# New priorities for the first blocks' operations, and maxima over partitions by a matmul whose stationary operand repeats the column

## The chip, the cores and the metric

The kernel runs on one core of one Trainium2 chip. The metric is the time of one execution on the device in microseconds (us), as the median of several runs. The engines are named as in the profile: PE is TensorE, DVE is VectorE, ACT is ScalarE, POOL is GpSimd, and SP is SyncE, which here only issues transfers.

## The reference

Three layers follow each other. The first is attention over keys and values that are averaged in groups of 8 positions, the second a dense two-layer network with a leaky activation, the third a network of 8 experts of which each token uses the one with the largest logit.

```python
# attention: B, H, S, D = 8, 8, 576, 64;  pool = 8;  Sp = 72
k_p = k.reshape(B, H, Sp, pool, D).mean(axis=3)
v_p = v.reshape(B, H, Sp, pool, D).mean(axis=3)
scores = scale * np.matmul(q, k_p.transpose(0, 1, 3, 2))
...
x = attn @ v_p                          # to (4608, 512)
h = x @ w_in                            # 512 -> 2048
g = np.maximum(h, 0.0) + alpha * np.minimum(h, 0.0)
x = g @ w_out                           # 2048 -> 512
...
logits = x @ w_gate                     # 8 experts
expert_idx = np.argmax(logits, axis=1)
...                                     # for each expert e and its tokens xe:
ye = np.maximum(xe @ w1[e], 0.0) @ w2[e]
out[mask] = gate_w[mask, None] * ye
```

## The kernel before

**Tiles and stages.** The 4608 tokens are 36 tiles of 128 and 18 blocks of two tiles. Every f32 operand of a large matmul is split into a high and a low f16 half, and three products of halves are added up. A split needs a power of two as a scale, and this needs a maximum over the operand. For a batch (`plan_batch`, 8 of them) K and V are loaded in slices into two buffers (`raw`), pooled (L450 on VectorE, L454 to L456 on GpSimd), scaled and split, and K is transposed by a DMA (`kT`, L483). For a tile (`plan_tile`) q is loaded, split and transposed by a DMA, then come scores (L572), maximum (`smax`), bias (`nb`, L583), exponentials (L591), a transposition by DMA (L622), the product with V (L631), and the split result xT. The tiles of the first two blocks need batch 0 alone; tile 4, the first of block 2, needs batch 1 too.

**The dense layer.** `plan_w` loads w_in and w_out in 8 chunks each, and puts each chunk together from integer parts (ScalarE L726 to L735, VectorE L738 and L742). It takes the chunk's maximum (L190), and once the maximum is there splits it into a high (`hi`) and a low half (`lo`, L210 on VectorE, L212 and L213 on GpSimd). w_in has four groups of two chunks with a scale each; w_out has one scale, so nothing of w_out is split before all 8 chunks have their maxima. `plan_in` computes a block's first layer (hp, L822: 16 parts of 12 matmuls), with the activation on ScalarE (L836) and VectorE (L840), and splits the result into gT. `plan_out` computes a tile's second layer (yp, L869: 4 parts of 12). Then come the gate and, beside all this, the scaling of the experts' weights (`plan_expert`). When the blocks are through, the expert slots follow (L1301, L1319).

**The maximum over partitions.** `over_all` (L308 to L332) takes a column with one maximum for each partition and returns the largest of the 128 in every partition. It masks the column to the bits of the exponent (L315), multiplies an identity matrix by it (`diag`, L320, VectorE, into the tile dg), and multiplies a matrix of ones with that diagonal on TensorE (L324, into the tile mp), so that every partition holds all 128 values. Then it reduces them (L327). It is called for alpha and the gate (a pair of columns), each batch (a pair; batch 0 in two calls), each w_in group, w_out, and each expert weight.

**The order of the work.** Nothing is issued as the program text runs. Each step is an operation of `Plan`, added with its engine or a choice of engines, an estimated duration, its inputs, a key and the buffers it takes and frees. `Plan.emit` plays the operations through with these estimates. At each step it takes, over all engines, the operation that can start first; among several that could start at the same time on an engine, the one with the smallest key goes first. The order found so is the order of each engine's queue. `PEN` is a handicap in us for each engine of a choice, and `lk` marks operations that share a port with GpSimd in the estimate. The operations are numbered in the order in which they are added. Keys of a block's first layer are 16j (j below 2) or 32j plus the part; `first` shifts some keys below 70.

## Time and profile before

| what | us |
|---|---|
| median of 3 runs | 1355.64 |
| lowest and highest of them | 1351.82, 1360.56 |
| the profiled execution | 1353.38 |
| its span, first to last instruction | 1351.7 |
| TensorE busy (91% of the span) | 1233.8 |
| VectorE busy (69%) | 935.2 |
| ScalarE busy (43%) | 585.4 |
| GpSimd busy (27%) | 361.8 |

The chain that ended last reaches back from the end only to 1011.67 us, through the expert slots' matmuls and scatters, so it tells nothing of the first blocks. The stages up to 300 us are read from tables by stage and from timelines. Wait times that are named behind an instruction are the idle time of its engine just before it, and what ended it.

### The profile page before, as it was taken

Reading aid. Unit: us, or ns where it says so; the run is one execution under the profiler, and the core shown is the slowest. Engines: PE = TensorE matmul, PEld = TensorE weight load, DVE = VectorE, ACT = ScalarE, POOL = GpSimd, SP = SyncE. Lnnn points to the kernel's source line nnn. Section 1 sums busy time; section 2 is a strip of 40 time slices with the busy share of each in tenths; the row PEclk is TensorE's granted clock in tenths of the full one; section 3 lists DMA queues with packets and bytes.
Section 4 is the critical chain, followed back from the end, with each engine's and each line's share of the span. In section 5 each row is a group of like instructions: output and inputs, shape, how many; then the busy total and the mean of one; then the engine's idle time right before and its main releaser. Section 6 shows DMA issues by size and latency. Waiting matters only on the chain. (4 is left out here: it accounts for less than half of the span.)

```text
span 1351.7 us, 30262 instructions
## 1 busy us (share of the span) xinstructions
PE 1233.8 (91%) x11555; PEld 862.0 (64%) x11555; DVE 935.2 (69%) x2268; ACT 585.4 (43%) x1342; POOL 361.8 (27%) x378
## 2 busy tenths in 40 slices
PE   0058599999999999999999999999999999999997
PEld 0046456657766776677657766776767677776775
DVE  6999998989998998989979976853432332322322
ACT  2797735556754665467546654731111110110100
POOL 4265233124244142112334202220211222121211
PEclk9998799999999999999999999999999999999999
DMA  9994386797887897987877678394489433883316
GB/s 236 281 238 134 71 214 199 158 209 198 217 184 161 219 210 148 215 158 178 220 179 203 144 188 180 78 298 132 111 238 251 84 84 74 251 267 72 86 49 216
DMA packets 314789, 237.71 MB, mean 176 GB/s; under 512 B 258383, under 2 KB 267727, under 8 KB 309776
## 3 DMA queue, kind: packets, MB, share of 16 engines
q1 hardware_dynamic: 301184, 215.46, 63.3%
q0 software_dynamic: 7552, 20.23, 4.8%
q8 instruction: 92, 1.51, 0.5%
q10 hardware_dynamic: 5904, 0.04, 0.3%
q14 instruction: 57, 0.47, 0.2%
HBM read 263.52 MB, written 54.87 MB: 236 GB/s over the span
## 5 line engine op out<-in xcount | busy, mean ns | idle before, releaser
L822 PE MATMUL hp<-xT,w_in_hl 128*128 128x256 f16 x3456 | 394.5, 275 | 6.8 <-DVE r L840 4.1
L869 PE MATMUL yp<-w_out_hl,gT 128*128 128x512 f16 x1728 | 383.9, 380 | 0.0
L822 PEld LDWEIGHTS <-w_in_hl 128*128 128x128 f16 x3456 | 335.8, 99 | 50.4 <-DVE r L840 4.6
L869 PEld LDWEIGHTS <-gT 128*128 128x128 f16 x1728 | 166.4, 98 | 193.3 <-issue 1.4
L1301 PEld LDWEIGHTS <-ws 128*128 128x128 f16 x3744 | 210.7, 98 | 5.8 <-issue 1.2
L1301 PE MATMUL hp<-x2gT,ws 128*128 128x128 f16 x3744 | 212.5, 219 | 1.0 <-ACT hr L1307 1.0
L1319 PE MATMUL op<-ws,ht 128*128 128x512 f16 x936 | 205.6, 379 | 0.5 <-issue 0.5
L1307 ACT ACTIVATE hr<-hp 128x512 f32<-128x512 f32 x78 | 46.2, 597 | 352.4 <-PE hp L1301 321.6
L1319 PEld LDWEIGHTS <-ht 128*128 128x128 f16 x936 | 90.5, 98 | 106.3 <-issue 0.9
L840 DVE SCALAR_TENSOR_TENSOR r<-r,al,hp 128x256 f32<-128x256 f32 x288 | 123.9, 471 | 8.6 <-ACT r L836 8.4
L1311 DVE CAST ht<-hr 128x512 f16<-128x512 f32 x78 | 33.7, 432 | 136.8 <-ACT hr L1307 135.1
L1326 DVE TENSOR_SCALAR so<-op,cb 128x512 f32<-128x512 f32 x39 | 29.3, 751 | 141.5 <-PE op L1319 138.2
L836 ACT ACTIVATE r<-hp 128x512 f32<-128x512 f32 x144 | 86.9, 604 | 90.0 <-PE hp L822 73.1
L591 ACT ACTIVATE e<-sc,nb,esc 128x72 f32<-128x72 f32 x288 | 116.4, 419 | 6.9 <-DVE inv L289 5.0
L195 ACT ACTIVATE eo<-ew,es 128x512 f16<-128x512 f32 x128 | 88.9, 723 | 65.3 <-DMA wsc<-eo 29.2
L1010 POOL DMA_INDIRECT table<-rec,pu x36 | 40.6, 1128 | 265.2 <-DVE pu L1007 142.0
L450 DVE TENSOR_REDUCE kp<-raw 72x64 f32<-72x512 f32 (+1 forms) x90 | 100.0, 1112 | 16.5 <-DMA raw<-in_k_dram 9.3
L848 ACT ACTIVATE gT<-r 128x512 f16<-128x512 f32 x144 | 91.5, 636 | 29.6 <-DVE r L840 15.8
L853 DVE TENSOR_TENSOR gT<-r,gT 128x512 f16<-128x512 f32 x142 | 100.7, 711 | 3.7 <-ACT gT L848 3.3
L1329 POOL DMA_INDIRECT out_dram<-so,srec x39 | 39.7, 1018 | 194.1 <-DVE cb L1324 93.9
L1276 POOL DMA_INDIRECT x2g<-x2d,srec x41 | 43.7, 1067 | 167.1 <-DMA srec<-table 61.3
L190 DVE TENSOR_REDUCE em<-ew 128x1 f32<-128x1024 f32 x64 | 76.7, 1206 | 0.0
(217 smaller groups left out, 1259.2 us busy)
## 6 DMA issues: line engine op xcount, KB each, us to landing
ws<-wsc SPq DMA_DIRECT2D x166, 1024.0 KB
ew<-in_moe_w_dram SPq DMA_DIRECT2D x32, 1024.0 KB
wsc<-eo SPq DMA_DIRECT2D x64, 512.0 KB
x2d<-x SPq DMA_DIRECT2D x36, 256.0 KB
qr<-in_q_dram SPq DMA_DIRECT2D x32, 256.0 KB
w_in_f<-in_moe_w_in_dram SPq DMA_DIRECT2D x16, 512.0 KB
w_out_f<-in_moe_w_out_dram SPq DMA_DIRECT2D x16, 512.0 KB
raw<-in_k_dram SPq DMA_DIRECT2D x56, 144.0 KB
```

Source lines behind the costliest of these rows:

```text
L190: V.tensor_reduce(out=o, in_=i, axis=axis, op=ALU.max, apply_absolute_value=True)
L195: A.activation(out=hi, in_=src, func=ACTF.Copy, scale=s)
L450: V.tensor_reduce(out=o_, in_=r.rearrange("p h (r d) -> p h d r", r=PL), axis=AX.X, op=ALU.add)
L591: A.activation(out=c["e"][x], in_=c["scv"][x], func=ACTF.Exp, bias=c["nb"][:, z // 4, z % 4:z % 4 + 1], scale=c["esc"], accum_out=c["sm"][x])
L822: T.matmul(out=hp, lhsT=wt[:, a, kk, (m % 4) * 128:(m % 4 + 1) * 128], rhs=xTt[j][:, x, kk, :], start=(n == 0), stop=(n == 3 * KD - 1))
L836: A.activation(out=c["r"], in_=hps[j, m // 2], func=ACTF.Relu, scale=-1.0)
L840: V.scalar_tensor_tensor(out=c["r"][:, z], in0=c["r"][:, z], scalar=al1[:, m - 1 + z:m + z], in1=hps[j, m // 2][:, z], op0=ALU.mult, op1=A ...
L848: A.activation(out=gT[j][0][:, n2], in_=c["r"], func=ACTF.Copy)
L853: on(eng).tensor_tensor(out=gT[j][1][:, n2], in0=c["r"], in1=gT[j][0][:, n2], op=ALU.subtract)
L869: T.matmul(out=ypt[i], lhsT=gT[j][x][:, m, o_ * 128:(o_ + 1) * 128], rhs=W["w_out"][part][:, w, m % 4, :], start=(m == 0 and x == 0 and w ...
L1301: T.matmul(out=hp[:, f, :], lhsT=ws[kk // 2][:, kk % 2, a, ff * 128:(ff + 1) * 128], rhs=c["xT"][:, x * KD + kk, :], start=(z == 0), stop= ...
L1319: T.matmul(out=op, lhsT=c["ht"][:, x, f, :], rhs=ws[f // 4][:, f % 4, w, :], start=(f == 0 and x == 0 and w == 0), stop=(f == KF2 - 1 and ...
```

## The change

**Keys and engines by number.** A table `KEYS` adds a shift to the keys of 92 operations, and `SIDE` fixes the engine of 9 that have a choice, by a handicap of 99 us on the others. The numbers count the operations of the new program, which has no `diag`. By the order of the calls they are these:

- 41 to 72: batch 1's loads of slices (keys down by about 5 to 7) and poolings. The poolings of K slices 2, 4, 5, 6 and 7 go from 14, 16, 17, 18 and 19 to 40.0, 44.8, 44.7, 36.8 and 31.0; those of V slices 3 to 6 from 23 to 26 up to 39.7 to 46.0; the last from 27 to 17.6. Each pooling also waits for the one before it, as in the old program.
- 80 to 137: a copy and V's low half of batch 1, loads and poolings of batches 2 and 3. 395 to 605: operations of tiles 1 to 9, among them splits of q, maxima, first exponentials and scales.
- 1321 to 1374: w_in's second chunk, two steps of its scales. 1412: the maximum of w_out's first chunk, 22 to 72.5. 1436 to 1448: w_out's sixth chunk, and the maximum over the chunks (27 to 15.9).
- 1472 to 1625: activations and splits of blocks 0 to 2, and the yp parts 2 and 3 of tile 2 (1576, 1577: 52 and 54 to 88.9 and 170.7). 1630 and 1631: yp parts of tile 4. 2478 to 2515: expert 0's loads, maxima, splits and a store. 2994 to 3036: gate matmuls and their reductions of blocks 0 and 1.
- `SIDE`: GpSimd for poolings of batches 2 and 3 (100, 112, 134), V's low half of batch 2 (130), the low half of w_out's second chunk (1457), and two splits of block 2 (1592, 1605); VectorE for one pooling of batch 1 (54) and one split of expert 0 (2506).

**The maximum over partitions.** `diag` and its tile go. The matmul takes as stationary operand the upper 16 bits of the masked f32 column, read as bf16 and repeated 128 times with step 0, and the identity as moving operand; a pair of columns takes two matmuls.

**Order between operations.** A q maximum waits, in the plan, for the scales of the tile four before. Scores and products of a tile that ends a batch come after those of all earlier tiles. The low halves of w_in and w_out follow each other, a block's last yp part comes after that of its first tile, and the store of x2d is dated from the split instead of the transpose before it.

```diff
@@ -34,8 +34,26 @@
+KEYS = {
+    11: 33.24, 41: -4.95, 43: -4.95, 45: -4.95, 46: 26.02, 47: -4.95, 49: -4.91, 50: 28.84, 51: -4.91, 52: 27.68, 53:
+    -6.76, 54: 18.82, 55: -6.76, 56: 12.02, 57: -6.8, 59: -6.8, 64: 16.68, 66: 22, 68: 16.98, 70: 18.33, 72: -9.43,
+    80: -3.31, 84: -9.06, 87: -4.35, 89: -4.35, 91: -5.5, 93: -5.75, 95: -2.35, 97: -2.82, 99: -2.27, 101: -2.27, 105:
+    -3.95, 110: 37.67, 115: 7.45, 118: 27.69, 119: 27.74, 124: 52.02, 130: -12.61, 137: -16.16, 395: 71.78, 401:
+    -57.07, 415: 27.13, 421: 66.26, 425: -127.75, 432: 4.88, 447: 71.14, 451: -3.83, 456: 63.31, 461: -25.55, 475:
+    9.79, 485: -124.46, 499: 59.65, 501: -8.17, 530: -68.36, 544: -72.1, 551: -64.63, 555: -18.52, 605: -33.03, 1321:
+    -101.78, 1322: -93.78, 1323: -60.6, 1365: 26.95, 1374: 25.36, 1412: 50.46, 1436: -101.23, 1437: -18.51, 1448:
+    -11.12, 1472: -1.09, 1487: 36.95, 1496: 37.83, 1555: 14.78, 1576: 36.9, 1577: 116.72, 1594: 9.08, 1625: 5.36,
+    1630: -94.27, 1631: -30.36, 2478: 137.61, 2481: 45.47, 2484: 27.95, 2495: -60.74, 2497: -51.38, 2498: 65.41, 2505:
+    -63.32, 2506: -125.52, 2507: -56.94, 2514: -13.19, 2515: 60.24, 2994: 46.2, 2996: -31.62, 2998: 45.68, 3036: 39.29
+}
+SIDE = {
+    54: "DVE", 100: "POOL", 112: "POOL", 130: "POOL", 134: "POOL", 1457: "POOL", 1592: "POOL", 1605: "POOL", 2506:
+    "DVE"
+}
 class Op:
-    __slots__ = ("eng", "dur", "fn", "deps", "key", "lat", "acq", "rel", "n", "users", "est", "end", "kind", "lk")
+    __slots__ = ("eng", "dur", "fn", "deps", "key", "lat", "acq", "rel", "n", "users", "est", "end", "kind", "lk", "pen")
@@ -50,7 +68,12 @@
         o = Op()
+        at = len(self.ops)
+        key += KEYS.get(at, 0)
         o.lk = lk
+        o.pen = PEN.get(eng)
+        if at in SIDE:
+            o.pen = tuple(0.0 if x == SIDE[at] else 99.0 for x in eng)
         o.kind = kind
@@ -94,7 +117,7 @@
                     if isinstance(o.eng, tuple):
-                        t += PEN[o.eng][o.eng.index(name)]
+                        t += o.pen[o.eng.index(name)]
                     if pick is None or (t, k, i) < pick[:3]:
@@ -250,7 +273,7 @@
     pools = dict(att=5, raw=2, kp=2, kc=1, KT=2, VS=2, vlo=1, q=3, qs2=1, qT=2, sc=1, e=2, A=1, AT=1, xT=2, wst=WST, wst2=WST2, big=15,
-                 h=3, r=2, y=2, x2=3, x2T=2, gps=1, dg=1, ew=4, eo=2, rec=3, so=2, srec=8)
+                 h=3, r=2, y=2, x2=3, x2T=2, gps=1, ew=4, eo=2, rec=3, so=2, srec=8)
     plan = Plan(pools)
@@ -314,21 +337,17 @@
-        def diag():
-            d["g"] = wk.tile([128, 2, 128], BF16, tag="dg", name="dg", bufs=1)
+        def mm():
+            h = get().bitcast(BF16)
+            d["p"] = ps_g.tile([128, 2, 128], F32, tag="g", name="mp")
             for z in range(n):
-                V.tensor_scalar(out=d["g"][:, z], in0=idb, scalar1=get()[:, z:z + 1], scalar2=None, op0=ALU.mult)
-        def mm():
-            d["p"] = ps_g.tile([128, 2, 128], F32, tag="g", name="mp")
-            T.matmul(out=d["p"][:, 0:n], lhsT=ones, rhs=d["g"][:, 0:n], start=True, stop=True)
+                T.matmul(out=d["p"][:, z], lhsT=h[:, 2 * z + 1:2 * z + 2].to_broadcast([128, 128]), rhs=idb, start=True, stop=True)
...
         o = chain("DVE", [mask], deps + [o_c1], key)
-        o = add("DVE", 0.17 * n, diag, [o], key=key, lat=0.05, acq=[("dg", 1)], lk=True)
-        o = add("PE", 0.07 * n, mm, [o], key=key - 1000, acq=[("gps", 1)], lat=0.15, rel=[("dg", 1)])
+        o = add("PE", 0.07 * n, mm, [o], key=key - 1000, acq=[("gps", 1)], lat=0.15)
         return add("DVE", 0.1 + 0.14 * n, red, [o], key=key - 1000, lat=0.05, rel=[("gps", 1)])
@@ -530,7 +549,7 @@
-    xTt, oX, oXh = {}, {}, {}
+    xTt, oX, oXh, oSC, oAV, oQM = {}, {}, {}, {}, {}, {}
     KC = (128, 3 * SP_ - 128)
@@ -643,16 +662,17 @@
         o = add("SP", dmat(262144) * 1.85, load, kind="q", key=first(dl - 30, -6), acq=[("q", 1), ("att", 1)])
-        o = add("DVE", dve(512), q1, [o], key=dl - 18)
+        o = add("DVE", dve(512), q1, [o], order=[oQM.get(i - 4)], key=dl - 18)
         o = chain("DVE", pow2s(lambda: (c["m"], c["inv"], c["s"])), [o], dl - 18)
-        o_s = o
+        o_s = oQM[i] = o
         o = add(ANY, his(512), q2, [o], key=dl - 17, acq=[("qs2", 1)], lk=True)
...
         o_e = add("DVE", tiny(len(bs)), esc, [o_s] + [oSK[b] for b in bs], key=dl - 13, lk=True)
-        o = add("PE", pe(16 * len(bs), SP_), scores, [o] + [oKT[b] for b in bs], key=dl - 13, acq=[("sc", 1)],
+        o = add("PE", pe(16 * len(bs), SP_), scores, [o] + [oKT[b] for b in bs], order=[oSC.get(x) for x in range(i) if ends], key=dl - 13, acq=[("sc", 1)],
                 rel=[("qT", 1)] + [("KT", 1)] * len(ends))
+        oSC[i] = o
         o = add("DVE", dve(576), smax, [o], key=dl - 12)
@@ -664,8 +684,9 @@
         o = add("SP", 1.8, aT, [o1, o2], kind="AT", key=dl - 7 - SPA, acq=[("AT", 1)], rel=[("A", 1)])
-        o = add("PE", pe(16, 128), av, [o] + [z for b in bs for z in oVS[b]], key=dl - 4, acq=[("gps", 1)],
+        o = add("PE", pe(16, 128), av, [o] + [z for b in bs for z in oVS[b]], order=[oAV.get(x) for x in range(i) if ends], key=dl - 4, acq=[("gps", 1)],
                 rel=[("AT", 1)] + [("VS", 1)] * len(ends))
+        oAV[i] = o
         o = oXh[i] = add("ACT", act(512), xhi, [o, oXh.get(i - 1)], key=dl - 3, acq=[("xT", 1)] if half == 0 else [])
@@ -784,7 +805,7 @@
-        p1 = None
+        p1 = p2 = None
         for c in range(8):
@@ -803,7 +824,7 @@
             o = p1 = add(ANY, his(1024), hi, [o_sc, p1], key=first(key - 1, 122), acq=[("big", 1)] if c % 2 == 0 else [], lk=True)
-            o = add(EITHER, stt(1024), lo, [o], key=first(key - 1, 91), rel=[("big", 1)] if c % 2 == 1 else [], lk=True)
+            o = p2 = add(EITHER, stt(1024), lo, [o], order=[p2], key=first(key - 1, 91), rel=[("big", 1)] if c % 2 == 1 else [], lk=True)
             oW[name] += [o, o]
@@ -870,7 +891,7 @@
             oY[i] = add("PE", pe(12, DM), mm, [oG[j, 2 * part], oG[j, 2 * part + 1]] + oW["w_out"][4 * part:4 * part + 4]
-                        + [oY.get(i) if part else None],
+                        + [oY.get(i) if part else None], order=[oY.get(i - 1) if last and o_ else None],
                         key=key_out(i) + 2 * part, acq=[("y", 1)] if part == 0 else [],
@@ -909,9 +930,10 @@
             o = add("DVE", dve(512), y3, [o], key=k_, rel=[("y", 1)])
+            o_y = o
             o = add("SP", 1.0, y4, [o], kind="yT", key=k_ - SPY, acq=[("x2T", 1)])
             oT.append(o)
-            oS.append(add("SP", dmat(262144), y5, [o], kind="x2", key=k_ + 1, rel=[("x2", 1)]))
+            oS.append(add("SP", dmat(262144), y5, [o_y], order=[o], kind="x2", key=k_ + 1, rel=[("x2", 1)]))
```

## Rows read from the trace of the kernel before

**Rows 1.** Page, 40 slices: busy tenths of TensorE.

```profile
PE   0058599999999999999999999999999999999997
```

**Rows 2.** By stage: length; PE, PEld, DVE, ACT, POOL busy; clock, DMA share, GB/s.

```profile
0.00:87.67 87.67, 7.98 (x103) 6.26 (x104) 71.07 (x125) 55.72 (x96) 35.61 (x48) 1.00 0.98 264
87.67:144.34 56.67, 49.77 (x423) 40.84 (x420) 55.14 (x106) 43.01 (x73) 29.86 (x24) 0.94 0.51 130
144.34:165.14 20.80, 4.56 (x99) 4.09 (x98) 19.93 (x47) 13.80 (x42) 3.52 (x3) 0.64 0.31 73
165.14:300.00 134.86, 132.78 (x967) 80.87 (x964) 122.47 (x290) 68.39 (x156) 34.30 (x34) 0.99 0.76 194
300.00:1351.70 1051.70, 1038.74 (x9977) 729.98 (x9975) 666.57 (x1703) 404.48 (x978) 258.50 (x271) 1.00 0.67 171
```

**Rows 3.** Timeline of TensorE: start, us, work, wait before.

```profile
87.67 7.63 PE L822 MATMUL hp<-xT,w_in_hl 128*128 128x256 f16 x48
...
127.22 17.19 PE L822 MATMUL hp<-xT,w_in_hl 128*128 128x256 f16 x156
...
144.34 1.12 PE L572 MATMUL sc<-KTb,qT 128*64 128x72 f16 x32
...
163.09 1.11 PE L572 MATMUL sc<-KTb,qT 128*128 128x72 f16 x16 [6.95 <-ACT e L591]
...
165.14 11.59 PE L869 MATMUL yp<-w_out_hl,gT 128*128 128x512 f16 x48
...
177.25 5.35 PE L869 MATMUL yp<-w_out_hl,gT 128*128 128x512 f16 x24
```

**Rows 4.** Timeline of VectorE, from the last w_out chunks to yp.

```profile
148.79 2.35 DVE L738 SCALAR_TENSOR_TENSOR w_out_t<-wc,w_out_t 128x1024 int32<-128x1024 int32 x2
...
154.31 0.10 DVE L315 TENSOR_SCALAR iw<-iw 128x1 int32<-128x1 int32 x1
...
155.58 0.24 DVE L320 TENSOR_SCALAR dg<-idb,iw 128x128 bf16<-128x128 bf16 x1
...
156.61 0.28 DVE L327 TENSOR_REDUCE mr<-mp 128x1 f32<-128x128 f32 x1
...
162.29 1.28 DVE L210 SCALAR_TENSOR_TENSOR w_out_hl<-w_out_t,cg,w_out_hl 128x1024 f16<-128x1024 f32 x1 [0.25 <-ACT w_out_hl L195]
```

**Rows 5.** Table by stage, the diagonal products of L320 alone.

```profile
0.00:165.14 165.14, 6.42 (x11) 0.93 0.74 194
165.14:1351.70 1186.56, 6.36 (x28) 1.00 0.68 173
```

**Rows 6.** Tiles dg and mp: min/median/max ns, first and last start.

```profile
L324 PE MATMUL mp<-dg,ones x31: 219/219/372, 19.1 to 851.9; 128*128 128x128 bf16 x23, 128*128 128x256 bf16 x8
...
L320 DVE TENSOR_SCALAR dg<-idb,m x16: 233/245/254, 202.7 to 849.2; 128x128 bf16<-128x128 bf16 x16
```

**Rows 7.** Batch 1's pooling on VectorE, and SyncE's transpose of its K.

```profile
L450 DVE TENSOR_REDUCE kp<-raw x15: 1008/1032/1054, 45.2 to 121.0; 72x64 f32<-72x512 f32 x15
...
138.49 1.36 SPq L483 DMA_TRANSPOSE KTb<-kc  x1
```

**Rows 8.** Timeline: tile 5's xT; a wait for a transpose in tile 0.

```profile
68.09 1.06 PE L631 MATMUL xp<-AT,VSb 128*64 128x128 f16 x16 [6.85 <-DMA AT<-Abuf]
...
179.17 0.67 DVE L210 SCALAR_TENSOR_TENSOR xT<-xp,xT 128x512 f16<-128x512 f32 x1
```

**Rows 9.** VectorE beside GpSimd (timelines); nb overall; GpSimd's low halves of w_out.

```profile
54.10 2.09 DVE L583 TENSOR_SCALAR nb<-mx,esc 128x8 f32<-128x8 f32 x1
...
53.66 2.50 POOL L213 TENSOR_TENSOR w_in_hl<-w_in_t,w_in_hl 128x1024 f16<-128x1024 f32 x1
...
L583 DVE TENSOR_SCALAR nb<-mx,esc x36: 211/222/2090, 41.7 to 858.6; 128x8 f32<-128x8 f32 x36
...
L212 POOL TENSOR_SCALAR w_out_t<-w_out_t,cg 128x1024 f32<-128x1024 f32 x2 | 7.9, 3968 | 14.8 <-ACT w_out_hl L195 14.8
...
L213 POOL TENSOR_TENSOR w_out_hl<-w_out_t,w_out_hl 128x1024 f16<-128x1024 f32 x2 | 4.3, 2132 | 0.2
```

## The prediction

> **What bounds the kernel now.** The slices of the page come first. TensorE is at nine tenths or more in nearly every slice from the sixth on [rows 1], so the end is set by TensorE once it runs without gaps, and the first slices set when it does. The table by stage says it in numbers [rows 2]: after 165.14 us TensorE is busy 132.78 of 134.86 us and 1038.74 of 1051.70 us. Before it there are 62.3 us of work in 165.14 us, so 102.8 us stand empty: 79.7 until the first block's first matmul, 6.9 from there to 144.34, and 16.2 in the stretch of 20.8 us that ends at 165.14. The granted clock is 0.94 in the second stretch and 0.64 in the third, in which TensorE was busy 4.56 of 20.80 us; later it is 0.99 to 1.00. A gain can come out of these 102.8 us and the slow matmuls among them. All that is empty after them is 15 us, part of it the wait for the last scatters.
>
> The order of TensorE's work around the hole is the third view [rows 3]. The first-layer matmuls (hp) of blocks 0 and 1 end at 144.4. From there only scores and attention products run, until the second-layer matmuls (yp) start at 165.14. What yp waits for is seen on VectorE [rows 4]: the last two w_out chunks are put together at 148.79. The mask follows at 154.31, the diagonal at 155.58, the maximum over partitions at 156.61, and the low half of the second chunk, the last thing that the first yp needs, ends at 163.57. VectorE is busy 71.1 of 87.7, 55.1 of 56.7 and 19.9 of 20.8 us in the three stretches [rows 2]. So in this phase the amount and the order of VectorE's work keep TensorE waiting.
>
> **The matmul with the column itself.** It takes the diagonal products away: 11 instructions, 6.42 us, before 165.14 and 28, 6.36 us, after it [rows 5]. The median of one is 0.245 us [rows 6], so the 11 would be 2.7 us; the rest of the 6.42 are two or so that took over 2 us, and such a wait may pass to the next instruction. The freed time lies between 2.7 and 6.42 us; I take 5, as many of its neighbours in the queue are reductions, and the pooling ones kept within 1.01 to 1.05 us [rows 7]. The 6.36 us after 165.14 are hidden by TensorE, 98% busy there; were VectorE the bound instead, they would be a gain of that size. The matmuls go from 31 to 39, since a pair of columns needs two. One takes 0.219 us, at most 0.372 [rows 6]; eight more are 1.8 to 3.0 us, and two of the eight (alpha with gate, batch 1) fall into TensorE's gaps before 165. The other six cost 0 to 1.3 us; I take 0.5. A stationary operand that repeats one column is not in the trace. At the least it loads as beside any matmul, at nothing; at the most its load is exposed and as long as a matmul of this size, 39 x 0.219 = 8.5 us. I take nothing, since the loads of other matmuls lie beside them.
>
> **Batch 1's pooling is moved back.** VectorE pools 15 of the 16 slices of batch 1's K and V between 45.2 and 121.0 us, 1.03 us each [rows 7]. The new keys put five K slices and four V slices from 16 to 26 up to 31 to 46, and the chain from slice to slice holds the others from the third on. The keys of blocks 0 and 1 lie between 2 and 34 and those of w_out's assembly and maxima between 22 and 38, so these now go first: that frees up to 13 x 1.03 = 13.4 us of VectorE ahead of yp. What hangs on the pooling (maximum, splits and copies for batch 1) is about another 4 us, by instructions of the same sizes as the rows show. The bounds are 0, if the time goes to work that isn't urgent, and 17 us. One term speaks for less: the maximum of w_out's first chunk gets key 72.5 and is left for a gap. I take a little over half, 9 us.
>
> What is late next is block 2. Its second tile's xT is written at 179.17 [rows 8]. It is not needed before the yp of blocks 0 and 1 are through: 24 of them take 5.35 us [rows 3], 192 take 42.8, so until 207.9. If yp starts at 151 they end at 194. Pooling and w_out only change places ahead of that tile, so its xT should come between 173 and 190. The earlier start isn't given back, but the margin falls from 28 us to between 4 and 21.
>
> **Work put on GpSimd.** Of seven operations pinned to it one matters, the low half of w_out's second chunk, which the first yp needs. On VectorE it took 1.28 us [rows 4]; on GpSimd the pair of instructions for such a chunk took 3.97 + 2.13 us on average [rows 9]. So 0, where attention work stands in front of yp anyway (scores waited 6.95 us for ScalarE there [rows 3]), to 4.8 us; I take 2. The other six, and two pinned to VectorE, lie behind a busy TensorE.
>
> What such pairings cost the other side is in the rows too. The scale for the exponentials (nb) takes 0.222 us in the median and 2.09 once, beginning at 54.10, while GpSimd ran a product from 53.66 that lasted 2.50 [rows 9]. The Trainium skill, SBUF — State Buffer, in "Who interferes with whom", has a rule for it: the two engines lock a shared pair of ports for a whole instruction, and the second stands still. The trace agrees, with those 2.09 us; by that rule products handed to GpSimd take back time on VectorE, and the sum would be rival (d) below.
>
> **Loads and the rest.** K and V loads of batches 1 and 2 come 2 to 7 key units earlier. The DMA share is 0.98 at 264 GB/s up to 87.67 [rows 2], so a slice of 144 KB ahead of a w_out load makes it 0.56 us later. There are two buffers for slices, held longer by late pooling, so hardly any can go ahead: 0 to 3 us, I take 1. The loads, maxima and scaling of expert 0's weights change places with each other and with this phase; the experts' weights last until 849 us [rows 6] and have room. Two parts of tile 2's yp get late keys: filler for later gaps, the same amount of work. The x2d store is planned earlier, behind a busy TensorE. Each of these costs nothing while TensorE stays busy; if its order of work blocks at a late input, they show as rival (c).
>
> **The clock.** 48 first-layer matmuls took 7.63 us at 87.67, where 156 took 17.19 at 127.22 [rows 3], or 5.3 for 48: 2.3 us lost. 6% of the second stretch of 56.67 us are 3.4 us. A start with fewer gaps gives back 0 to 3.4; I take 1.
>
> **The sum.** Ahead of yp 5 + 9 = 14 us are freed, and the clock gives 1. Against it stand 2 for the low half, 1 for loads and 0.5 for matmuls: 11.5 us, for which the hole of 16.2 has room. The profiled execution took 1353.4 us (span 1351.7 and 1.7 around it), 2.2 under the median of the runs, 1355.6. From it I get 1353.4 - 11.5 = 1341.9, so 1342. A measurement of this kernel tells about 1% from no change, and 1% under the median is 1342.1: the forecast stands on that border.
>
> **The rivals.** (a) More. The first block starts earlier too, as tile 1's chain runs through the same VectorE queue. Then the hole's 16.2 us, 5 of the gaps before it and 3.4 of the clock go: 1353.4 - 25 = 1328. Against it: this chain also waits for transposes (6.85 us for one [rows 8]) that no order on VectorE shortens.
>
> (b) The hole only moves. w_out is ready a little earlier, but the scores in front of yp, the first chunk's late maximum or the low half on GpSimd hold it. The diagonals' 2.7 to 6.4 us are left of the gain: about 1349. For it speaks the wait of 6.95 us in front of yp.
>
> (c) Slower: block 2 comes late. It decides when tile 5's xT comes after 194. If pooling is put off until w_out is through at 151, its 13.4 us take 22 at six tenths of VectorE's time, then as now 17.5 us from the last slice (121.0) to the transpose of K (138.49) [rows 7] and 41.4 to xT (179.84): 232, a hole of 38 us. 1353.4 - 11.5 + 38 = 1380. Against it: VectorE has time to pool whenever w_out waits for ScalarE or for a load, and the pooling then starts before 151.
>
> (d) GpSimd's extra work blocks VectorE: three of the seven operations come before or near yp, and 2.09 - 0.22 = 1.9 us each would cost 6 of the 11.5 us: 1348. The port rule above is this rival. Against it: the median of 36 nb is 0.222 us [rows 9], though GpSimd is busy 69.0 of the 165.1 us [rows 2].
>
> **How the numbers follow.** Forecast, 1334 to 1346: 0.46. (a), 1320 to 1334: 0.18. (b), 1346 to 1358: 0.18, and (d), in the same span: 0.08. (c), over 1360: 0.10. Faster by over 1% is (a) and some six tenths of the forecast: 0.46. Slower by over 1% is most of (c): 0.09. Within 1%: 0.45. The range leaves out the lower third of (a), all of (c) and a little of (b): 1325 to 1358.
>
> **What would show it.** Right: no diagonal products; most of batch 1's pooling after 100 us; w_out's maximum over partitions near 145 instead of 156.6; yp from about 153; no gap of over 8 us before it; the rest of the span as long as before. Wrong: yp at 160 or later (b), a new gap between 185 and 250 with block 2's hp waiting for xT (c), more VectorE instructions of 2 us beside GpSimd's (d), or a first hp well before 87 (a).

## The result, and the profile after

The changed kernel took 1365.66 us in the median of 20 runs (1360.14 to 1378.12), the kernel before 1358.20 us in as many on the same chip (1351.82 to 1360.73). The ratio is 1.006, with a 95% interval of 1.0043 to 1.0077: slower by 0.6%. The forecast was 1342, the range 1325 to 1358. Both the size and the direction were wrong. The profiled execution took 1366.16 us, with a span of 1364.5. The profile of the kernel before (1353.38 us) is of an execution 4.8 us under that kernel's median, so the two profiles lie 12.8 us apart and the two medians 7.5. The account below is of the two profiles.

The table by stage of the changed kernel (stretch, its length, then busy us and instructions of TensorE, its weight loads, VectorE, ScalarE and GpSimd, then the granted clock, the DMA share and GB/s):

```profile
0.00:165.14 165.14, 74.02 (x594) 54.57 (x595) 145.16 (x253) 110.70 (x182) 79.50 (x89) 0.92 0.73 187
165.14:300.00 134.86, 132.87 (x1069) 84.87 (x1068) 118.10 (x299) 74.31 (x200) 32.65 (x46) 1.00 0.82 201
300.00:900.00 600.00, 584.24 (x4902) 396.67 (x4901) 520.47 (x1329) 339.75 (x858) 153.62 (x162) 0.99 0.75 175
```

The same view of the kernel before, from 300 to 900 us:

```profile
300.00:900.00 600.00, 595.69 (x5082) 410.42 (x5081) 524.16 (x1374) 350.58 (x887) 177.10 (x193) 1.00 0.77 183
```

The first 165 us went as forecast: TensorE is busy 74.02 us there, where it was 62.3 [rows 2]. The middle row stands as before. The loss is in the third: TensorE idles 15.8 us between 300 and 900 us, where it idled 4.3.

The timeline of TensorE in the changed kernel (start, length, line, tiles, form, count, and in brackets the idle time before it with what ended it):

```profile
79.08 0.37 PE L843 MATMUL hp<-xT,w_in_hl 128*128 128x256 f16 x1 [1.51 <-ACT xT L218]
...
138.52 0.22 PE L344 MATMUL mp<-idb,iw 128*128 128x128 bf16 x1
...
147.56 7.09 PE L890 MATMUL yp<-w_out_hl,gT 128*128 128x512 f16 x24
...
158.53 1.12 PE L591 MATMUL sc<-KTb,qT 128*64 128x72 f16 x16 [3.25 <-DMA KTb<-kc]
...
293.26 1.47 PE L843 MATMUL hp<-xT,w_in_hl 128*128 128x256 f16 x12
...
943.62 2.56 PE L1323 MATMUL hp<-x2gT,ws 128*128 128x128 f16 x43
```

The two of these points in the kernel before that its rows ahead of the prediction do not have, block 4's first hp matmul and the first expert matmul:

```profile
300.72 1.48 PE L822 MATMUL hp<-xT,w_in_hl 128*128 128x256 f16 x12
930.95 10.88 PE L1301 MATMUL hp<-x2gT,ws 128*128 128x128 f16 x192
```

This gives the whole account. The first hp is at 79.08 (87.67 before [rows 3]) and the first yp at 147.56 (165.14 before). Block 4 (192 hp matmuls a block, counted off the trace) starts 300.72 - 293.26 = 7.5 us ahead. From there to the first expert matmul it took 943.62 - 293.26 = 650.4 us, where the kernel before took 930.95 - 300.72 = 630.2: 20.1 us lost. The experts take as long as before, 1364.5 - 943.6 = 420.9 against 420.8. So 7.5 us were won and 20.2 lost, which is the difference of the two spans, 12.8, but for rounding.

The table by stage, cut at these points, tells idle time from slower work. The kernel before comes first:

```profile
0.00:300.72 300.72, 195.80 (x1596) 132.66 (x1597) 269.33 (x569) 181.64 (x366) 103.92 (x109) 0.96 0.75 194
300.72:930.95 630.23, 625.92 (x5263) 428.39 (x5260) 535.00 (x1408) 356.62 (x897) 178.51 (x194) 1.00 0.76 187
```

```profile
0.00:293.26 293.26, 200.15 (x1599) 133.39 (x1600) 256.68 (x528) 180.19 (x361) 110.54 (x131) 0.95 0.75 192
293.26:943.62 650.36, 632.62 (x5269) 430.41 (x5265) 546.81 (x1409) 358.24 (x899) 164.73 (x173) 0.99 0.77 182
```

TensorE's instructions are as many as before but for a few. Ahead of block 4 it idles 93.1 us instead of 104.9, 11.8 less, and its work takes 4.4 us longer (200.15 against 195.80). From block 4 to the experts it idles 17.7 us instead of 4.3, 13.4 more, and its work takes 6.7 us longer (632.62 against 625.92).

What TensorE waited for between 300 and 900 us, changed kernel (engine, tile, line, what it waited for: us in total, times, longest):

```profile
PE gp L955 <- DMA x2T<-x: 8.7, 7, 2.9
PE xp L650 <- DMA AT<-Abuf: 3.6, 3, 2.5
PE hp L843 <- DVE xT L233: 1.7, 2, 0.8
```

The kernel before, same view:

```profile
PE xp L631 <- DMA AT<-Abuf: 3.3, 2, 3.1
PE hp L822 <- DVE inv L289: 0.6, 1, 0.6
```

The gate's matmuls (gp) wait for the DMA transpose that writes x2T. Before, they never waited in this stretch. The transposes' issue on SyncE, with the kernel before first (count, then ns at the least, in the median and at the most):

```profile
L902 SPq DMA_TRANSPOSE x2T<-x x28: 1232/1269/2840, 299.5 to 892.9; - x28
```

```profile
L923 SPq DMA_TRANSPOSE x2T<-x x25: 1232/1447/4558, 298.9 to 858.9; - x25
```

Eight of the 25 took over 2 us to issue, where 1 of 28 did. Counted by single issues on SyncE, 1281 KB of copies were issued in the 5 us ahead of an x2T transpose on average, 655 of them loads of expert weights; before the change it was 707 KB with 37 of expert loads. The planner gives the expert loads earliest times of their own (`x.est = EXP0 + EXPD * (2 * e + w)`, every 46 us), which the new keys don't move, while the blocks around them come earlier. The first theory was that these loads make the transposes late.

At the end of three waits the granted clock fell: two for x2T (2.85 us until 308.25, 2.54 until 683.82) and one of 2.47 us for AT (until 843.31). The stretches around the first, and at the second and the third, columns as in the table by stage:

```profile
300.00:308.00 8.00, 5.40 (x56) 4.76 (x54) 5.08 (x12) 6.90 (x14) 1.14 (x2) 1.00 0.95 198
308.00:311.50 3.50, 3.25 (x30) 2.50 (x31) 2.83 (x9) 0.79 (x2) 0.99 (x1) 0.52 0.24 59
311.50:320.00 8.50, 8.50 (x81) 6.51 (x78) 6.99 (x25) 5.53 (x20) 0.22 (x1) 1.00 0.42 84
683.40:687.00 3.60, 3.18 (x23) 2.36 (x24) 2.76 (x7) 1.02 (x5) 0.00 (x0) 0.53 1.55 356
843.90:847.30 3.40, 3.40 (x13) 1.20 (x10) 1.35 (x2) 1.18 (x2) 0.00 (x0) 0.50 0.01 4
```

So of the 20.1 us, 13.4 are idle time and 6.7 are the same work run more slowly. The three stretches at half the clock explain about 5 of the 6.7 (half of the 3.2 to 3.4 us that TensorE was busy in each). About 2 us weren't placed.

### The profile page after: what moved, and what is told of

The parts are those of the page before. It is cut to its first block, busy times and chain, and to the rows that moved or that the text cites. A ratio compares the mean times of both kernels' runs of the same rounds, so it can differ in the third digit from the quotient of the medians.

```text
span 1364.5 us, 30219 instructions
## 1 busy us (share of the span) xinstructions
PE 1244.9 (91%) x11563; PEld 864.9 (63%) x11563; DVE 934.7 (69%) x2228; ACT 585.5 (43%) x1340; POOL 355.2 (26%) x380
## 4 chain that ended last, share of the span: by engine, by line
PE 66%; DMA 13%; DVE 11%; issue 5%; ACT 2%; SPq 1%; POOL 1%; ACTq 1%; POOLq 0%; DVEq 0%
PE yp L890 18%; PE hp L843 16%; PE hp L1323 15%; PE op L1341 14%; DMA x2T<-x 2%; DMA raw<-in_k_dram 2%; DMA raw<-in_v_dram 2%; DMA AT<-Abuf 2%; DVE r L861 1%; DVE m L213 1%; PE xp L650 1%; PE sc L591 1%; DVE kp L469 1%; DMA qr<-in_q_dram 1%; DMA out_dram<-so,srec 1%
## 5 line engine op out<-in xcount | busy, mean ns | idle before, releaser
L843 PE MATMUL hp<-xT,w_in_hl 128*128 128x256 f16 x3456 | 399.2, 276 | 17.8 <-DVE r L861 8.4
L890 PE MATMUL yp<-w_out_hl,gT 128*128 128x512 f16 x1728 | 389.6, 383 | 1.4 <-DVE inv L308 1.4
L861 DVE SCALAR_TENSOR_TENSOR r<-r,al,hp 128x256 f32<-128x256 f32 x288 | 123.6, 471 | 13.1 <-ACT r L857 11.8
L469 DVE TENSOR_REDUCE kp<-raw 72x64 f32<-72x512 f32 (+1 forms) x86 | 96.0, 1117 | 20.8 <-DMA raw<-in_k_dram 12.8
```

Of the source, the lines that this page charges most:

```text
L469: V.tensor_reduce(out=o_, in_=r.rearrange("p h (r d) -> p h d r", r=PL), axis=AX.X, op=ALU.add)
L843: T.matmul(out=hp, lhsT=wt[:, a, kk, (m % 4) * 128:(m % 4 + 1) * 128], rhs=xTt[j][:, x, kk, :], start=(n == 0), stop=(n == 3 * KD - 1))
L861: V.scalar_tensor_tensor(out=c["r"][:, z], in0=c["r"][:, z], scalar=al1[:, m - 1 + z:m + z], in1=hps[j, m // 2][:, z], op0=ALU.mult, op1=A ...
L890: T.matmul(out=ypt[i], lhsT=gT[j][x][:, m, o_ * 128:(o_ + 1) * 128], rhs=W["w_out"][part][:, w, m % 4, :], start=(m == 0 and x == 0 and w ...
```

## The experiments

Ratios are to the kernel before, run beside each on the same chip. "300 to 900" is TensorE's busy time in that stretch, which is 595.69 before and 584.24 after the change.

### One part alone, with nothing moved

The kernel before, with the maxima by the column itself, all other operations in exactly the order that they had. The replay of a fixed order is the same in every experiment that says so:

```diff
     def emit(self):
-        ... (plays the operations through with keys and estimates)
+        left = [(int(x[:-1]), "SPADQ".index(x[-1])) for x in ORDER.split()]
+        while left:
+            for n, (i, a) in enumerate(left):
+                o = self.ops[i]
+                if o.n == 0 and all(free[p] >= c for p, c in o.acq):
+                    break
...
-            T.matmul(out=d["p"][:, 0:n], lhsT=ones, rhs=d["g"][:, 0:n], start=True, stop=True)
+            for z in range(n):
+                T.matmul(out=d["p"][:, z], lhsT=h[:, 2 * z + 1:2 * z + 2].to_broadcast([128, 128]), rhs=idb, start=True, stop=True)
```

> The kernel before with only the maximum over partitions changed (column as stationary operand, no diagonal), and with the order of all other operations on every engine kept as it was in the kernel before. It measures the matmul alone. If the diagonal's time counts (6.4 us of VectorE before the first second-layer matmul), the time falls by 2 to 6 us against the kernel before: ratio 0.996 to 0.998. If the loss of the changed kernel comes from the repeated column itself, it rises: ratio over 1.003.

Measured: 1361.3 us against 1360.29, ratio 1.0016 (0.9986 to 1.0047), 300 to 900 at 594.71. The matmuls in this kernel (ns at the least, in the median and at the most):

```profile
L451 PE MATMUL mp<-idb,kvm x16: 219/219/287, 16.0 to 743.0; 128*128 128x128 bf16 x16
L451 PE MATMUL mp<-idb,m x16: 219/219/219, 205.3 to 858.8; 128*128 128x128 bf16 x16
```

The other seven of the 39, all ahead of 156 us, took up to 311 ns; with the matrix of ones one took 372 [rows 6]. A stationary operand that repeats a column costs nothing extra. But the diagonals' time isn't gained either: VectorE is busy 142.56 us ahead of 165.14 instead of 146.14, and yet yp starts at 166.41, no earlier than before. The interval leaves room for 2 us of gain or 6 of loss, but the trace doesn't show the changed kernel's loss: from block 4 to the experts this kernel took 632.9 us, near the 630.2. So the matmul is neither the forecast's gain nor, by the trace, the loss.

This replay is also a second profile of the old order, from an execution in the middle of its runs (1361.59 us). Block 4 starts at 304.53 in it. Against it the changed kernel is 11.3 us ahead at block 4 and loses 17.5 us from there, where it was 7.5 and 20.1 against the fast profile.

### The new order up to block 3, then the old one

```diff
 ORDER: operations as the changed kernel issues them up to block 3's first hp,
+       then those that are left, as the kernel before issues them
```

> The changed kernel's order up to the first operation of block 3's first layer, and from there all that is left in the order of the kernel before; column matmul throughout. Theory A (the start is a real gain of some 7 us, and the later blocks lose it through another order on the queues): 1347 to 1353 us, ratio about 0.993 to 0.996. Theory B (work that the start put off comes back later whatever the order): 1358 to 1368, ratio 1.000 or more, with gaps on TensorE after 300 us as in the changed kernel.

Measured: 1366.76 us, ratio 1.0054 (1.0024 to 1.0084). By stage:

```profile
165.14:300.00 134.86, 119.54 (x930) 75.55 (x929) 111.11 (x278) 68.23 (x176) 32.66 (x45) 0.95 0.75 188
300.00:900.00 600.00, 594.58 (x5027) 404.71 (x5026) 523.46 (x1348) 349.55 (x882) 172.25 (x190) 1.00 0.74 181
```

For the total it is inconclusive: the seam of two orders tore a hole of its own (7.7 us of hp waiting for the activation's buffer r near 269). The second row tells something, though. After the new start, the old order of the later blocks lost nothing: 941.1 - 308.1 = 633 us from block 4 to the experts, near the 630.2 of before and the 632.9 of the replay. What costs some 20 us is how the changed kernel orders its later blocks.

### Is it the x2d store's place?

In the changed kernel the store of x2d often stands right behind the transpose. Two kernels: the first one above with the store put there, and the changed kernel with the store two transfers later (both replay a fixed order).

```diff
 ORDER (first kernel of this section):  x2T transpose, ..., x2d store
+                                       x2T transpose, x2d store, ...
 ORDER (changed kernel):                x2T transpose, x2d store, a, b
+                                       x2T transpose, a, b, x2d store
```

> The same as the kernel with the frozen order and the column matmul, but each store of x2d stands directly behind the transpose of the same tile in SyncE's queue, as in the changed kernel, instead of 1 to 5 transfers later. Theory C (the store behind the transpose makes x2T late, so that the gate matmuls hold TensorE's queue): slower than the frozen order by 5 to 15 us, with several waits for x2T on TensorE after 300 us. Theory A without this cause: within 3 us of the frozen order.

> The changed kernel with its order kept on every engine, except that each store of x2d goes two transfers later into SyncE's queue. Theory C: the waits for x2T after 300 us go and 6 to 14 us come back, ratio to the kernel before 0.995 to 1.001. If the store isn't the cause: ratio 1.004 to 1.008 as measured for the changed kernel.

Measured: 1363.66 us, ratio 1.0030 (0.9999 to 1.0060), with no wait for x2T; and 1374.14 us, ratio 1.0079 (1.0051 to 1.0107), with more of them:

```profile
PE gp L1085 <- DMA x2T<-x: 14.9, 8, 3.2
```

Neither move did what this theory says: the store's place isn't the cause.

### Is it the expert loads right ahead of the transposes?

The changed kernel's order, with 17 of the 32 expert loads moved from up to 6 us ahead of an x2T transpose to right behind it.

```diff
 ORDER:  expert load, (up to 6 us), x2T transpose
+        x2T transpose, expert load
```

> The changed kernel with its order kept on every engine, except that 17 loads of expert weights (1 MB each), which stand in SyncE's queue up to 6 us by the plan ahead of a transpose of x2T, stand right behind it. Theory D (in the changed kernel the expert loads, whose due times are fixed and were not moved with the blocks, fall just ahead of the gate's transposes; these land late and the gate matmul holds TensorE's queue): most of the 8.7 us of waits for x2T go, and the time falls by 6 to 14 us against the changed kernel, ratio to the kernel before 0.995 to 1.001. If the transposes' lateness is not what costs: 1.004 to 1.008.

Measured: 1367.89 us, ratio 1.0045 (1.0019 to 1.0070). The copies ahead of the transposes fell from 1281 to 614 KB, the expert loads among them from 655 to 41, and yet:

```profile
PE gp L1085 <- DMA x2T<-x: 6.6, 3, 3.7
PE xp L780 <- DMA AT<-Abuf: 5.1, 3, 3.5
PE hp L973 <- DVE xT L363: 2.4, 1, 2.4
```

300 to 900 stands at 582.53, and block 4 to the experts took 654.9 us. The waits changed their names and kept their sum (17.5 us of idle time between 300 and 900, where it was 15.8). So the narrow theory, that loads directly ahead of x2T are the whole cause, falls.

### The expert loads' earliest times, planned anew

One constant, which the change doesn't touch, is shifted, and the planner deals the order again. Only `-18` differs from kernel to kernel:

```diff
-            x.est = EXP0 + EXPD * (2 * e + w)
+            x.est = EXP0 + (-18) + EXPD * (2 * e + w)
```

> The changed kernel, planned anew with the earliest time of every expert load 18 us earlier, about as much as the blocks were moved in the plan, so that loads and transposes stand to each other as in the kernel before. Theory D: ratio to the kernel before 0.990 to 0.997. If another feature of the later order is the cause: 1.003 to 1.009.

> The same with 24 us. The transfers issued just ahead of x2T fall further, but the last blocks come later in the plan. Theory D says that x2T is hardly waited for and the time lies near or under the kernel before, 0.992 to 1.000. The rival, that the plan's own end decides, says that it is slower than with 18 us by 10 us or more.

> The kernel before, planned anew with the earliest time of every expert load 18 us later and nothing else changed. By the plan this puts as much expert traffic ahead of the x2T transposes as in the changed kernel. Theory D: slower than the kernel before by 5 to 15 us, ratio 1.004 to 1.011, with waits for x2T on TensorE after 300 us. Otherwise: 0.997 to 1.003.

> The changed kernel planned anew with the expert loads' earliest times 20 us earlier. Theory E (what counts is how the expert traffic stands in the period of a block; 18 us back restores it): ratio to the kernel before 0.990 to 0.997, no stretch of low clock between 300 and 900 us. Theory F (the gain with 18 us was luck of one order; any small change gives another order, good or bad): anywhere from 0.990 to 1.009.

> The same with 16 us earlier. Theory E: 0.990 to 0.999, though the plan's own end is 8 us later than with 18. Theory F: anywhere from 0.990 to 1.009.

> The same with 2 us earlier, so nearly the changed kernel. Theory E: as slow as the changed kernel, 1.002 to 1.010, with waits of 2 us and more for transposes after 300 us. Theory F: anywhere from 0.990 to 1.009.

> The same with 2 us later. Theory E: 1.002 to 1.010. Theory F: anywhere from 0.990 to 1.009.

> The changed kernel with the expert loads' earliest times 18 us earlier, a second time with more rounds, since it was the fastest of several shifts and may have been picked for a lucky measurement. If the gain is real: 0.990 to 0.996. If it was luck of the measurement: 0.997 or more, as with 16 and 20 us.

> The changed kernel planned anew with the expert loads' earliest times 18 us later. By the plan the transfers issued within 6 us ahead of a transpose of x2T fall from 1165 KB (tiles 6 to 35, changed kernel) to 652. Theory E (their place in the period of a block decides): ratio 0.990 to 1.000 and few waits for x2T. If only loading the experts earlier helps, whatever the place in the period: 1.003 to 1.012.

"Block 4 to experts" is the time from block 4's first hp to the first expert matmul. The waits are TensorE's from 300 us to the experts. "KB ahead" is what was issued in the 5 us ahead of an x2T transpose on average, with the expert loads' part behind it. The trace columns are from one execution of each kernel; at -2 it was the slowest of ten (1377.54 us), which lost its extra time only behind the last block.

| kernel, shift in us | us | ratio (95%) | 300 to 900 | block 4 to experts, us | waits for x2T, us | KB ahead of x2T, expert loads |
|---|---|---|---|---|---|---|
| changed, -24 | 1358.78 | 0.9971 (0.9947 to 0.9995) | 590.02 | 642.3 | 2.4 | 554, none |
| changed, -20 | 1358.56 | 0.9985 (0.9963 to 1.0006) | 596.00 | 636.8 | 3.8 | 766, none |
| changed, -18 | 1350.40 | 0.9925 (0.9893 to 0.9957) | 596.23 | 630.0 | 1.9 | 843, 152 |
| the same, a second time | 1346.69 | 0.9910 (0.9878 to 0.9942) | 595.86 | 632.1 | 0.6 | 834, 146 |
| changed, -16 | 1358.45 | 0.9988 (0.9964 to 1.0012) | 592.26 | 633.5 | 0.8 | 581, none |
| changed, -2 | 1366.90 | 1.0035 (1.0008 to 1.0062) | 582.64 | 651.1 | 6.8 | 1133, 591 |
| changed, 0 | 1365.66 | 1.0060 (1.0043 to 1.0077) | 584.24 | 650.4 | 8.7 | 1281, 655 |
| changed, +2 | 1374.21 | 1.0104 (1.0067 to 1.0142) | 576.67 | 654.9 | 10.4 | 1162, 551 |
| changed, +18 | 1352.21 | 0.9955 (0.9931 to 0.9978) | 595.02 | 638.1 | none | 656, none |
| before, +18 | 1356.66 | 0.9972 (0.9937 to 1.0007) | 595.95 | 631.0 | 1.5 | 926, 417 |

The stretch and the waits at -18, and the waits at +2:

```profile
300.00:900.00 600.00, 596.23 (x5084) 410.79 (x5082) 524.84 (x1365) 349.26 (x872) 158.42 (x174) 1.00 0.73 183
```

```profile
PE gp L955 <- DMA x2T<-x: 1.9, 1, 1.9
PE xp L650 <- DMA AT<-Abuf: 1.1, 1, 1.1
```

```profile
PE gp L955 <- DMA x2T<-x: 10.4, 6, 3.9
PE hp L843 <- ACT xT L218: 4.8, 1, 4.8
```

With -18 the new start is worth what was forecast. Block 4's first hp, and the first expert matmul:

```profile
291.35 1.91 PE L843 MATMUL hp<-xT,w_in_hl 128*128 128x256 f16 x16
...
921.31 1.89 PE L1323 MATMUL hp<-x2gT,ws 128*128 128x128 f16 x31
```

That is 630.0 us, as long as before (630.2), and both points come 9.4 to 9.6 us earlier. The second profile of the same kernel has block 4 at 297.19, only 3.5 us earlier, and 632.1 us from there, so a single profile places the start only within some 6 us. In the two measurements the time is 1361.44 - 1350.40 = 11.0 us and 1359.32 - 1346.69 = 12.6 us under the kernel before, where the prediction's sum was 11.5. That it agrees so closely is partly luck, as the terms of that sum didn't come out one by one. This version beats both kernels.

Three things came out that the first theory doesn't give. The time isn't smooth in the shift: -20 and -16 give away what -18 keeps. At -16 block 4 starts only at 304.06, since an mp matmul waits 8.4 us for xT near 300 (TensorE is busy 125.55 us between 165 and 300, and 132.21 at -18). At -20 it starts at 297.51, and 3.8 us go on an x2T transpose near 905. Earlier isn't the point: +18 comes to 0.9955, although its block 4 to experts is 8 us longer than at -18. At -24 the time is 8.4 us over that at -18, a little short of the 10 of the rival that lets the plan's own end decide. And the kernel before, shifted by +18, wasn't slower; but the shift brought only 417 KB of expert loads ahead of its transposes, not the 655 of the changed kernel, so it is a weak test.

What goes together in the rows of the changed kernel is 651 to 655 us from block 4 to the experts (650.4 unshifted), waits for x2T of 6 us and more, over 1 MB ahead of these transposes with over 500 KB of expert loads in it, and under 585 us of TensorE's time: shifts -2, 0 and +2 have all of these, the others none. The sum of KB alone doesn't predict the wait: 926 KB cost 1.5 us in the kernel before with +18, and 614 KB cost 6.6 in the kernel with 17 loads moved. Of the two theories in the expectations, E (the place of the expert traffic in a block's period) missed at -20, which came out at 0.9985 against 0.990 to 0.997, and was met at -16, -2, +18 and, but for 0.0004, at +2. F (another order, another luck) fits nearly every outcome and isn't excluded.

### The matmul alone, planned anew

The kernel before with the diagonals taken out and no keys, and the planner left to deal the order.

```diff
-        o = add("DVE", 0.17 * n, diag, [o], key=key, lat=0.05, acq=[("dg", 1)], lk=True)
-        o = add("PE", 0.07 * n, mm, [o], key=key - 1000, acq=[("gps", 1)], lat=0.15, rel=[("dg", 1)])
+        o = add("PE", 0.07 * n, mm, [o], key=key - 1000, acq=[("gps", 1)], lat=0.15)
```

> The kernel before with the column matmul alone, planned anew (no new keys, no fixed engines, no new order between operations). With the order kept it was 1.0016. If planning anew alone deals the later blocks a different order with its own luck, this differs from 1.0016 by 0.003 or more to either side; if the later order hardly changes without new keys, 0.998 to 1.004.

Measured: 1373.35 us, ratio 1.0116 (1.0065 to 1.0167). By stage:

```profile
165.14:300.00 134.86, 125.92 (x950) 77.56 (x949) 121.83 (x288) 70.95 (x171) 36.47 (x32) 0.98 0.71 188
```

The same edit with the order kept was at 1.0016. The planner's new deal alone, in answer to 39 short instructions that are gone, costs 1% (four runs, 1365.33 to 1378.02 us, of which the fastest was profiled). In this profile TensorE idles 8.9 us between 165 and 300, where it idled 2.1, and block 4 starts 9.7 us later than before. Nothing is lost in the later blocks (633.0 us from block 4 to the experts).

## Why the prediction was wrong, point by point

**What bounds the kernel: right.** TensorE sets the end once it runs, and a hole ahead of yp was there to be closed.

**The hole ahead of yp: right, and undersized.** w_out's maximum over partitions ran on TensorE at 138.52 (forecast near 145, before 155.88), and yp began at 147.56 (forecast 153). 38 yp matmuls were through by 165.14, 8.4 us of work, while hp stood at 384 as before. The first hp came 8.6 us earlier, which rival (a) had named. So the first yp came 17.6 us earlier and block 4 7.5 us: of the idle time ahead of block 4, 11.8 us went, where the sum without its clock term has 10.5, and 4.4 us came back as slower work.

**The clock, 1 us gained: wrong in sign.** Between the first hp and the first yp (79.08 to 147.56) TensorE is busy 51.10 us at a granted clock of 0.88; in as long a stretch from the first hp on (87.67 to 156.15) it was busy 52.28 us at 0.91 before. Up to block 4 the same work takes 4.4 us longer, where the forecast had 1 less.

**Diagonals, 5 us: not shown.** They are gone, but alone they gave nothing with the order kept. In the changed kernel VectorE is busy 145.16 us before 165.14, where it was 146.1 [rows 2]: its time was filled. That the gain came from the order follows from this; no run has the new order with the diagonals.

**Pooling, 9 us: right in direction, by another way in part.** Of batch 1's 16 slices ten are pooled after 107 us, 4 on VectorE and 6 on GpSimd (from 118.14 to 135.29); GpSimd has taken nine in all, where VectorE had 15 [rows 7]. The prediction had put the work later on VectorE.

**Low half on GpSimd, 2 us: it fits, but isn't measured apart.** Timeline of GpSimd, VectorE and TensorE in the changed kernel:

```profile
143.89 1.25 POOL L235 TENSOR_SCALAR w_out_t<-w_out_t,cg 128x1024 f32<-128x1024 f32 x1 [1.43 <-ACT w_out_hl L218]
...
145.22 2.13 POOL L236 TENSOR_TENSOR w_out_hl<-w_out_t,w_out_hl 128x1024 f16<-128x1024 f32 x1
...
146.04 1.33 DVE L338 TENSOR_SCALAR kvm<-kvm 128x2 int32<-128x2 int32 x1
...
147.43 0.33 PE L344 MATMUL mp<-idb,kvm 128*128 128x128 bf16 x2 [2.14 <-DVE inv L308]
```

The low half ended at 147.35, and the first yp followed at 147.56; hp had ended at 145.28. But the matmul of batch 1's maximum stands in front of yp in TensorE's queue, and it waited until 147.43 for the third row, which ended at 147.37. So the low half and rival (d) held yp to the same moment.

**Rival (d): its sign is there, its price is small.** The third row took 0.15 us in the kernel before and ends with GpSimd's instruction, 146.04 + 1.33 = 147.37. Another stands at 17.82: 2.24 us for a one-column product beside GpSimd's from 17.71 on. The rule on the shared ports in the Trainium skill, SBUF — State Buffer, "Who interferes with whom" (the engine that comes second stands still for the whole instruction of the first), agrees with both: 1.2 and 2.1 us more. Ahead of 300 us VectorE has five instructions of over 2 us beside GpSimd's, the long poolings aside, where it had four. They didn't make the later blocks' loss. The one at 17.82 also shows what the bound of the diagonals had allowed: in the kernel before a diagonal took 2.30 us in this place (at 16.78, beside GpSimd's from 16.69 on), and its wait passed to the next small instruction.

**Rival (c): in small.** Scores waited 3.25 us at 158.53 for batch 1's K, pooled late. There was no hole between 165 and 300 (132.87 us busy, 132.78 before [rows 2]).

**"The rest of the span as long as before": wrong, and this is the step that failed.** The sum moved the end by all that the start gains and took the later order as given. But the keys go into the same planner that deals every operation after them, and 7.5 us at block 4 came with 20.1 us lost before the experts: 13.4 of idle time and 6.7 of slower work, for which the sum had no term. No rival had a place behind 250 us; an order that "blocks at a late input" was sent to rival (c), which priced block 2 alone. The prediction had the clue in its own words: an edit there "costs nothing while TensorE stays busy", and whether TensorE stays busy under a new order was not asked. With the same start and the expert loads 18 us earlier, the forecast's step holds (630.0 and 632.1 against 630.2 us) and the time is at 1346.69 to 1350.40.

**What is shown and what isn't.** Shown: the loss isn't in the matmul (632.9 us from block 4 to the experts with it alone), nor in the new start as such (633 with it and the old later order, 630.0 and 632.1 at -18); it comes with the order that the planner deals to the later blocks. Its visible form is TensorE waiting for DMA transposes, x2T's for 8.7 us of it, and running at half its clock after three such waits. Not settled: which feature of that order makes the transposes late. Expert loads ahead of x2T mark the three slow shifts, but moving 17 of them behind the transposes by hand kept the loss, and the kernel before bore 417 KB of them. The change's own rules of order (for q maxima, for scores and products, for yp and for the x2d store) also hold in the later blocks and weren't taken out one by one; at -18 they all hold and nothing is lost, so they don't force the loss.

## What to carry to other kernels

When an order is dealt by a planner, a change of keys at one place is a new order everywhere behind it, and a forecast needs a term for that: here one changed kernel came out between 0.991 and 1.0104 of the kernel before by shifts of one constant, and the matmul alone at 1.0016 in the old order and at 1.0116 in a new one. Test an edit with the rest of the order held fixed before it is credited or blamed. And when the start of a pipeline moves, look for times written in absolute units, such as the loads' earliest times, and try a few of them anew.

## What the hardware showed that was not expected

- A matmul whose stationary operand repeats one column ran in 0.219 us (median), like one with a full matrix. In the changed kernel its weight load took 95 to 107 ns, 98 in the median; with the matrix of ones it took 97 to 139 ns, also 98 in the median.
- An x2T transpose takes 1.23 to 1.27 us to issue in half of the cases in the kernel before; in the changed kernel the median is 1.45 us and the longest 4.6, where some of them stand behind many copies on SyncE's queue (5.6 at shift +2, but 5.3 once in each profile at -18 too, where TensorE's waits for x2T came to 1.9 and 0.6 us in all).
- In the changed kernel's later blocks three waits of 2.5 to 2.9 us of a TensorE that was otherwise busy were each followed by some 3.4 us in which the granted clock was 0.50 to 0.53, the lower of its two levels (1.2 GHz of 2.4). This isn't so for every such wait: in the kernel before, one of 3.07 us was followed by a clock of 1.00.

```profile
704.48 0.66 PE L631 MATMUL xp<-AT,VSb 128*64 128x128 f16 x16 [3.07 <-DMA AT<-Abuf]
```
